# Two column groups of the last mixing sum in two-bank PSUM tiles, tile 32 in halves, five residual buffers, and a new order of the jobs

## The chip, the cores and the metric

The kernel runs on one core of a Trainium2 chip. Its time is the device time of one execution in microseconds; the time shown for the kernel before is the median of three runs. The profile is that of one more execution.

The names of the engines are those of the profile: PE is TensorE (PEld its weight loads), DVE VectorE, ACT ScalarE, POOL GpSimd, SP SyncE, which issues nearly all DMAs here.

## The reference

Two layers follow each other: a retention layer (attention with a decay in place of the softmax) over 8 batches, 8 heads, 576 positions and 64 dimensions a head, then a gated MLP with a mixing sum along the sequence.

```python
scores = scale * np.matmul(q, k.transpose(0, 1, 3, 2))
Dmat = np.where(rel >= 0, gamma[:, None, None] ** rel[None, :, :], 0.0)   # rel = pos[:, None] - pos[None, :]
attn = np.matmul(scores * Dmat[None], v)
x = attn.transpose(0, 2, 1, 3).reshape(B, S, H * D)      # (8, 576, 512)
h = gelu_tanh(x @ w_in)                                  # (8, 576, 1024)
u, v = h[..., :512], h[..., 512:]
v_n = (v - mean(v)) / np.sqrt(var(v) + 1e-06) * g_ln
v_s = np.einsum('ts,bsd->btd', w_sg, v_n) + b_sg[None, :, None]
out = x + (u * v_s) @ w_out
```

Inputs and output are float32.

## The kernel before

**Tiling.** Two batches form a pair (index p, 0 to 3). A pair has 1152 rows, nine tiles of 128 rows (index m; tile number i = 9p + m, 0 to 35). The retention layer runs in blocks (index b, five to a pair, 0 to 19): blocks of 256 positions of one batch, and one block in the middle of each pair (b mod 5 = 2) with the last 64 positions of the first batch and the first 64 of the second. Matmuls are in bf16, sums in float32 PSUM.

**The jobs.** The kernel is cut into some 940 jobs, each a short function on one engine. Those of a block are: loads of q, k and v (a_load, SP; q mostly for two blocks at once); scaling of q and v by powers of gamma and a cast of k (a_prep, POOL, but DVE and ACT for block 0); transposes of q and k on PE with a copy by DVE (a_T, a_Tev), or by DMA for the later blocks (a_TX, SP); scores (a_S, PE) and their product with a mask (a_Sev, DVE); the state K'V (a_Z, PE), its running sum (a_Zsum, DVE) and its copy (a_Zev, ACT); the output in two steps (a_O1 and a_O2, PE) and its copy to xT (a_Oev, ACT).

For each tile then: v = x w_in (m_V, PE), gelu (m_Vg, ACT), mean and variance (m_stats, DVE), reciprocal root (m_rs, POOL), normalising (m_norm, ACT); u = x w_in (m_U, PE) with gelu (m_Ug, ACT); for each batch bt and each of four column groups c the mixing sum (m_Wm opens it with the 64 rows of the shared middle tile, m_W adds four tiles; PE, each in two halves of 288 positions), its gate u * (sum + b) (m_Wg, DVE, a half at a time); at last the product with w_out (m_O, PE), the sum with the residual x (m_Oev, DVE) and the store (m_store, SP). The residual x of a tile is xT transposed back: on PE with a copy by ACT for the nine tiles of the first pair (m_XT, m_XTev), by DMA for the others (m_X).

**The order.** One constant (ORDER, L20 to L54) lists the numbers of the jobs in the order in which their instructions are issued; fN in it is a fill of N/2 matmuls on a tile of zeros (L210 to L217). Each engine executes its own jobs in this order and waits, in order, for what a job needs. So ORDER is the schedule of every engine and of the DMA queue of SP.

**Buffers.** BUFS (L126) gives their numbers: among others eight for loads (ld), four for output tiles (ob), two for the residual that PE transposes (xt). PSUM has eight banks: psP has two tiles of two banks each (transposes, scores and block outputs, tag pp), psD has four tiles of one bank (all others, tag d). The two halves of a mixing sum take two psD tiles.

**The opening.** rsrc (g_ln and b_sg) is transposed (to_col, L742) and worked on by DVE (col_math, L747 to L750); its result colr scales w_sg (ACT, L272, five jobs), which is then transposed on PE (build_wT, L760, ten jobs). w_in comes in two halves, each cast by DVE (L246) and ACT (L248). The load of w_sg reuses the buffer of the first half of w_in and so stands behind both casts. Before the change, SP loads q, k of block 0, q of block 1, v of block 0, k of block 1, the first half of w_in, v of block 1, the last rows of w_sg, q and k of block 2; the only fill is f4, ahead of the first build_wT.

**The end.** The last batch is bt = 7. Its four column groups run in the order c = 1, 2, 3, 0, each m_Wm directly ahead of its m_W. Then come tiles 34, 33, 35 (in two halves of 256 columns, L690 and L1004), 31 and 32.

The lines of the mixing sum:

```python
for half in range(2):
    cur["wp", b, c, half] = psD.tile([128, HS], F32, name="wp", tag="d")
```

Of the kernel before, what the change touches and what calls it, by code (L numbers as in the profile page):

```python
# [11 lines left out]
F32 = mybir.dt.float32  # L12
# [81 lines left out]
def kernel(  # L94
# [32 lines left out]
                xr=5, xt=2, pp=2, d=4)  # L127
# [530 lines left out]

    def m_Wm(b, c):
        p, e = divmod(b, 2)  # L660
        for half in range(2):
            cur["wp", b, c, half] = psD.tile([128, HS], F32, name="wp", tag="d")
        for g in range(2):
            for half in range(2):
                R, G = slice(64 * half, 64 * half + 64), slice(64 * g, 64 * g + 64)
                mid = vns[NT * p + MID] if half == e else vsw[p]
                nc.tensor.matmul(cur["wp", b, c, half][G, :], mid[R, 128 * c + 64 * g:128 * c + 64 * g + 64], wM[e][R, :],  # L667
                                 start=True, stop=False, skip_group_check=True)

    def m_W(b, c):  # L670
        p, e = divmod(b, 2)
        t0 = NT * p + (MID + 1 if e else 0)
        for half in (1, 0):
            ps = cur["wp", b, c, half]
            for j in range(MID):
                ins = nc.tensor.matmul(ps[:], vns[t0 + j][:, 128 * c:128 * c + 128], wT[e][:, j, half * HS:(half + 1) * HS],  # L676
                                       start=False, stop=(j == MID - 1), skip_group_check=True)
                if half and j == 0:
                    mark(ins, ("W", b, c))
        fence(ins, ("W", b, c))  # L680

    def m_Wg(b, c, half):
        p, e = divmod(b, 2)
        o = e * S + half * HS
        dst = uTs[p][:, c, o:o + HS]
        ins = nc.vector.scalar_tensor_tensor(dst, cur.pop(("wp", b, c, half))[:], colr[:, c:c + 1], dst, op0=Alu.add, op1=Alu.mult)  # L686
# [3 lines left out]
    LAST = NT * NP - 1  # L690
# [190 lines left out]
    for b in range(NBL):  # L881
# [77 lines left out]
        if n in (2, NBK - 1):  # L959
# [10 lines left out]
            for u in order:  # L970
                due = base + PR["WS"] * cum / tot
                if u[0] == "W":
                    c = u[1]
                    cum += 1090.0
                    db = Buf("d"), Buf("d")
# [8 lines left out]
                    for hf in range(2):  # L984
                        J["Wg", bt, c, hf] = add("DVE", 450.0, due + 400.0, lambda a=(bt, c, hf): m_Wg(*a),
                                                 deps=[jW] + list(dict.fromkeys(J["Ug", i, c] for i in tls)),
                                                 uses=[db[hf], B_u])
                else:
# [15 lines left out]
                    for hf in (0, 1) if i == LAST else (None,):  # L1004
# [38 lines left out]
```

## Time and profile before

| | |
|---|---|
| median of three runs | 207.51 us |
| the three runs | 204.18, 207.51, 210.31 us |
| the profiled execution | 206.49 us |
| its span | 204.8 us |
| PE busy | 182.8 us (89%) |
| DVE busy | 159.8 us (78%) |
| POOL busy | 115.6 us (56%) |
| ACT busy | 110.1 us (54%) |
| DMA | 50.47 MB, mean 246 GB/s |

The span is the time from the first to the last event of the profiled execution. An engine is busy while one of its instructions runs; waiting and the issue of DMAs are not counted. PE's matmuls are pipelined, so that the length of one row is longer than its share in a stream of them: a stream is read from the start of its first row to the start of the next group.

### The profile page before, as it was taken

How to read it: one execution, taken by the hardware profiler on the slowest of the kernel's cores; microseconds unless marked ns; L12 is line 12 of the kernel's file. 1: busy time of each engine (PE TensorE's matmuls, PEld its weight loads, DVE VectorE, ACT ScalarE, POOL GpSimd, SP SyncE). 2: the span in 40 equal slices, each digit the busy share in tenths (PEclk: the TensorE clock that was granted, in tenths of full speed). 3: DMA queues.
4: the chain of work that ended last, by engine and by line, in shares of the span. 5: the costliest groups of instructions: out<-in, count | busy, mean ns of one | idle time of the engine just before them, and what ended most of it. 6: DMA issues, size and time to landing. Idle time of an engine off the chain costs nothing.

```text
span 204.8 us, 7667 instructions
## 1 busy us (share of the span) xinstructions
PE 182.8 (89%) x3267; PEld 121.9 (60%) x3295; DVE 159.8 (78%) x295; ACT 110.1 (54%) x197; POOL 115.6 (56%) x163
## 2 busy tenths in 40 slices
PE   0336898999999999999999999999999999999992
PEld 0335384876765777757656776556656676656550
DVE  3459686898998999799965867789796678966673
ACT  4322769646866854788464685634346467054200
POOL 8457079949797979966576695217068253202000
PEclk9999999999999999999999999999999999999999
DMA  5996999899999992979999979999999979583735
GB/s 167 348 366 159 358 360 300 256 327 287 299 327 239 333 352 55 196 228 345 331 291 166 210 227 187 198 221 243 326 367 147 270 174 241 156 157 110 223 105 207
DMA packets 94239, 50.47 MB, mean 246 GB/s; under 512 B 45360, under 2 KB 87612, under 8 KB 94204
## 3 DMA queue, kind: packets, MB, share of 16 engines
q1 hardware_dynamic: 94176, 49.97, 93.2%
q8 instruction: 26, 0.43, 0.8%
q14 instruction: 9, 0.07, 0.1%
q10 hardware_dynamic: 28, 0.01, 0.0%
HBM read 32.79 MB, written 9.44 MB: 206 GB/s over the span
## 4 chain that ended last, share of the span: by engine, by line
PE 70%; DVE 11%; DMA 7%; POOL 6%; issue 2%; ACT 1%; SPq 1%; DVEq 0%; POOLq 0%
PE wp L676 15%; PE hu L638 13%; PE op L701 12%; PE hv L597 12%; PE pp L532 5%; PE pp L450 4%; DVE ret L463 4%; DMA ld<-in_q_dram 3%; POOL qb L362 3%; PE wp L667 3%; DMA kT<-kb 3%; PE pp L399 2%; PE zp L486 2%; POOL vb L362 2%; DMA out_dram<-ob 1%
## 5 line engine op out<-in xcount | busy, mean ns | idle before, releaser
L362 POOL TENSOR_TENSOR vb<-ld,gpow 128x1024 bf16<-128x1024 f32 (+1 forms) x20 | 34.5, 1731 | 14.1 <-DMA ld<-in_v_dram 14.1
L463 DVE TENSOR_TENSOR ret<-pp,msk 128x1024 bf16<-128x1024 f32 x32 | 38.7, 1218 | 3.8 <-PE pp L450 3.6
L597 PE MATMUL hv<-w_in,xT 128*128 128x512 bf16 x127 | 36.0, 385 | 1.6 <-ACT xT L586 0.4
L638 PE MATMUL hu<-xT,w_in 128*128 128x256 bf16 (+1 forms) x320 | 36.2, 262 | 0.2 <-ACT zb L518 0.2
L676 PE MATMUL wp<-wT,vn 128*128 128x288 bf16 x256 | 36.4, 287 | 0.0
L686 DVE SCALAR_TENSOR_TENSOR uT<-wp,colr,uT 128x288 bf16<-128x288 f32 x64 | 30.4, 509 | 7.4 <-PE wp L676 7.3
L627 ACT ACTIVATE vn<-vg,mv 128x512 bf16<-128x512 f32 x36 | 28.7, 809 | 12.6 <-POOL mv L620 12.5
L701 PE MATMUL op<-w_out,uT 128*128 128x512 bf16 (+1 forms) x137 | 34.8, 373 | 0.7
L604 ACT ACTIVATE vg<-hv 128x512 f32<-128x512 f32 x36 | 21.2, 596 | 25.0 <-PE hv L597 16.5
L362 POOL TENSOR_TENSOR qb<-ldq,gpow 128x1024 bf16<-128x1024 f32 x14 | 26.5, 1902 | 10.9 <-DMA ldq<-in_q_dram 10.9
L638 PEld LDWEIGHTS <-w_in 128*128 128x128 bf16 x320 | 28.1, 98 | 7.2 <-issue 0.4
L586 ACT ACTIVATE xT<-pp 128x512 bf16<-128x512 f32 (+1 forms) x40 | 20.5, 550 | 20.2 <-PE pp L532 20.1
L612 DVE BATCH_NORM_STATS2 bst<-vg 128x6 f32<-128x512 f32 x36 | 24.6, 684 | 4.9 <-ACT vg L604 4.8
L676 PEld LDWEIGHTS <-vn 128*128 128x128 bf16 x256 | 22.8, 98 | 8.3 <-issue 0.9
L617 POOL TENSOR_SCALAR mv<-mv 128x2 f32<-128x2 f32 (+1 forms) x20 | 4.8, 240 | 38.0 <-DVE mv L613 31.1
L648 ACT ACTIVATE uT<-hu 128x512 bf16<-128x512 f32 x36 | 20.9, 594 | 8.1 <-PE hu L638 7.9
L730 DVE SCALAR_TENSOR_TENSOR ob<-op,col,xr 128x512 f32<-128x512 f32 (+1 forms) x28 | 20.1, 728 | 6.0 <-PE op L701 5.5
L701 PEld LDWEIGHTS <-uT 128*128 128x128 bf16 x148 | 13.9, 98 | 13.1 <-DVE uT L686 0.4
L597 PEld LDWEIGHTS <-xT 128*128 128x128 bf16 x144 | 13.3, 99 | 13.2 <-ACT xT L586 1.3
L618 POOL TENSOR_TENSOR mv<-mv,mhalf 128x2 f32<-128x2 f32 (+1 forms) x20 | 13.7, 685 | 1.7
L352 POOL CAST kb<-ld 128x1024 bf16<-128x1024 f32 x14 | 14.3, 1037 | 0.6 <-DMA ld<-in_k_dram 0.6
L532 PE MATMUL pp<-qT,zb 64*64 64x128 bf16 (+1 forms) x256 | 11.6, 222 | 1.1 <-DVE ret L463 0.3
(85 smaller groups left out, 221.9 us busy)
## 6 DMA issues: line engine op xcount, KB each, us to landing
out_dram<-ob SPq DMA_DIRECT2D x35, 256.0 KB, 2.9
ld<-in_k_dram SPq DMA_DIRECT2D x16, 512.0 KB, 7.5
ld<-in_v_dram SPq DMA_DIRECT2D x16, 512.0 KB, 5.9
ldq<-in_q_dram SPq DMA_DIRECT2D x7, 1024.0 KB, 7.9
xT<-in_moe_w_sg_dram SPq DMA_DIRECT2D x2, 576.0 KB, 3.4
ld<-in_q_dram SPq DMA_DIRECT2D x2, 512.0 KB, 4.9
xT<-in_moe_w_in_dram SPq DMA_DIRECT2D x1, 1024.0 KB
ld<-in_q_dram SPq DMA_DIRECT2D x8, 128.0 KB, 5.5
```

The source lines that it names most:

```text
L362: ve.tensor_tensor(dst, src, g.unsqueeze(len(src.shape) - 1).to_broadcast(list(src.shape)), op=Alu.mult)
L463: ins = nc.vector.tensor_tensor(ret[:].rearrange("p r (k t) -> p (r k) t", k=2), sc[:].rearrange("p r (k t) -> p (r k) t", k=2), (msk2 if ...
L532: nc.tensor.matmul(ot[64 * c:64 * c + 64, bank, j * cs:(j + 1) * cs], lhsT, rhs, start=(bank, c) not in begun, stop=True, skip_group_check ...
L597: ins = nc.tensor.matmul(hv[:], xTs[p][:, m, kk, :], w_in[:, kk, F2:], start=(kk == 0), stop=(kk == KK - 1))
L604: unfence(nc.scalar.activation(vgs[i][:], cur.pop(("hv", i))[:], Act.Gelu_apprx_tanh), ("V", i))
L612: nc.vector.bn_stats(bst[:], vgs[i][:])
L627: nc.scalar.activation(vns[i][:], vg[:], Act.Identity, scale=mv[:, s, 2:3], bias=mv[:, s, 3:4])
L638: ins = nc.tensor.matmul(hu[:, n, :], w_in[:, kk, 128 * c:128 * c + 128], xTs[p][:, m:m + w, kk, :], start=(kk == 0), stop=(kk == KK - 1), ...
L648: unfence(nc.scalar.activation(uTs[p][:, c0:c1, 128 * m:128 * m + 128 * w], cur.pop(("hu", i, half))[:], Act.Gelu_apprx_tanh), ("U", i, half))
L676: ins = nc.tensor.matmul(ps[:], vns[t0 + j][:, 128 * c:128 * c + 128], wT[e][:, j, half * HS:(half + 1) * HS], start=False, stop=(j == MID ...
L686: ins = nc.vector.scalar_tensor_tensor(dst, cur.pop(("wp", b, c, half))[:], colr[:, c:c + 1], dst, op0=Alu.add, op1=Alu.mult)
L701: ins = nc.tensor.matmul(op[:], uTs[p][:, c, r], w_out[:, c, cs], start=(c == 0), stop=(c == KK - 1), skip_group_check=True)
```

## The change

In the last batch (bt = 7) the column groups c = 1 and c = 2 no longer take two one-bank tiles each but one two-bank tile of psP, one half in each bank, and one DVE instruction of 128 x 576 gates both halves. Their m_Wm stand further ahead in the order: before the O2 of block 19, and between the m_W of (6, 1) and the m_Wm of (6, 3). Tile 32 leaves in two halves of 256 columns like tile 35, with a job each for matmul, sum and store. The residual transposed by PE has five buffers in place of two. ORDER is new throughout; since the number of jobs changed, its numbers name other jobs from the last batch on.

In the new order of the opening, SP loads q, k, v of block 0, then q, k of block 1, the first half of w_in, q, k of block 2, v of block 1, the last rows of w_sg, v of block 2. A fill f14 (seven matmuls) is PE's first job and f6 stands behind block 0's scores; f4 is gone. POOL prepares v of block 0 first, then q and k of block 1, q and k of block 2, v of 1 and 2. DVE does the column math directly behind the first transposed copy, and the cast of w_in behind the transposed copy of block 1. On ACT four of the five w_sg scalings stand behind the copy of the state (1, 0), with the copies of the state and of the output of block 2 between them.

At the end PE works W(7, 1), the openers of (7, 0) and (7, 3), W(7, 2), W(7, 3), W(7, 0), then tiles 32 (two halves), 31, 34, 35 (two halves), 33. The gate of (7, 0) does half 0 first; before, it did half 1 first.

```diff
 ORDER = (
...
+    '0 f14 1 2 95 6 7 96 73 3 98 97 99 12 74 187 188 100 259 13 189 f6 260 262 190 263 101 8 261 103 264 104 265 17 '
...
     BUFS = dict(ld=8, ldq=2, qb=2, kb=2, vb=3, qT=2, kT=2, ret=4, zb=6, run=4, xT=2, uT=2, vg=3, mv=3, vn=14, ob=4,
-                xr=5, xt=2, pp=2, d=4)
+                xr=5, xt=5, pp=2, d=4)
...
+    WPP = ((2 * NP - 1, 1), (2 * NP - 1, 2))
+
     def m_Wm(b, c):
         p, e = divmod(b, 2)
+        if (b, c) in WPP:
+            cur["wp", b, c] = psP.tile([128, 2, 512], F32, name="pp", tag="pp")
         for half in range(2):
-            cur["wp", b, c, half] = psD.tile([128, HS], F32, name="wp", tag="d")
+            cur["wp", b, c, half] = (cur["wp", b, c][:, half, :HS] if (b, c) in WPP else
+                                     psD.tile([128, HS], F32, name="wp", tag="d")[:])
...
     def m_Wg(b, c, half):
         p, e = divmod(b, 2)
+        if half is None:
+            dst = uTs[p][:, c, e * S:e * S + S].rearrange("p (a w) -> p a w", a=2)
+            unfence(nc.vector.scalar_tensor_tensor(dst, cur.pop(("wp", b, c))[:, :, :HS], colr[:, c:c + 1], dst,
+                                                   op0=Alu.add, op1=Alu.mult), ("W", b, c))
+            return
...
-    LAST = NT * NP - 1
+    LAST = (NT * NP - 1, NT * NP - 4)
...
-                    db = Buf("d"), Buf("d")
+                    db = (Buf("pp"),) if (bt, c) in WPP else (Buf("d"), Buf("d"))
...
-                    for hf in range(2):
-                        J["Wg", bt, c, hf] = add("DVE", 450.0, due + 400.0, lambda a=(bt, c, hf): m_Wg(*a),
...
+                    if (bt, c) in WPP:
+                        J["Wg", bt, c, 0] = J["Wg", bt, c, 1] = add(
+                            "DVE", 770.0, due + 400.0, lambda a=(bt, c, None): m_Wg(*a),
+                            deps=[jW] + list(dict.fromkeys(J["Ug", i, c] for i in tls)), uses=[db[0], B_u])
+                    else:
+                        for hf in range(2):
+                            J["Wg", bt, c, hf] = add("DVE", 450.0, due + 400.0, lambda a=(bt, c, hf): m_Wg(*a),
...
-                    for hf in (0, 1) if i == LAST else (None,):
+                    for hf in (0, 1) if i in LAST else (None,):
```

The numbers 450.0 and 770.0 in it are weights of jobs that nothing reads any more; only ORDER decides.

More of the change, by code (lines that the diff above doesn't have):

```diff
@@ L675, in m_W @@
             for j in range(MID):
-                ins = nc.tensor.matmul(ps[:], vns[t0 + j][:, 128 * c:128 * c + 128], wT[e][:, j, half * HS:(half + 1) * HS],
+                ins = nc.tensor.matmul(ps, vns[t0 + j][:, 128 * c:128 * c + 128], wT[e][:, j, half * HS:(half + 1) * HS],
                                        start=False, stop=(j == MID - 1), skip_group_check=True)
@@ L683, in m_Wg @@
         p, e = divmod(b, 2)
+        if half is None:
[3 more added lines that the diff above has]
+            return
         o = e * S + half * HS
         dst = uTs[p][:, c, o:o + HS]
-        ins = nc.vector.scalar_tensor_tensor(dst, cur.pop(("wp", b, c, half))[:], colr[:, c:c + 1], dst, op0=Alu.add, op1=Alu.mult)
+        ins = nc.vector.scalar_tensor_tensor(dst, cur.pop(("wp", b, c, half)), colr[:, c:c + 1], dst, op0=Alu.add, op1=Alu.mult)
         cur["leftw", b, c] = cur.get(("leftw", b, c), 2) - 1
         unfence(ins, ("W", b, c), cur["leftw", b, c] == 0)
-    LAST = NT * NP - 1
+    LAST = (NT * NP - 1, NT * NP - 4)
     def m_O(i, hf=None):
@@ L983 @@
                     J["W", bt, c] = jW
-                    for hf in range(2):
-                        J["Wg", bt, c, hf] = add("DVE", 450.0, due + 400.0, lambda a=(bt, c, hf): m_Wg(*a),
-                                                 deps=[jW] + list(dict.fromkeys(J["Ug", i, c] for i in tls)),
-                                                 uses=[db[hf], B_u])
+                    if (bt, c) in WPP:
[5 more added lines that the diff above has]
+                            J["Wg", bt, c, hf] = add("DVE", 450.0, due + 400.0, lambda a=(bt, c, hf): m_Wg(*a),
+                                                     deps=[jW] + list(dict.fromkeys(J["Ug", i, c] for i in tls)),
+                                                     uses=[db[hf], B_u])
                 else:
```

65 rows, old and new, of the table ORDER are left out of this document.

## The prediction

> **What bounds the kernel now.** I read the busy times of stretches first, since an average over the span mixes three regimes. Columns: stretch, its length, busy us of PE, PEld, DVE, ACT and POOL, granted TensorE clock, DMA share, GB/s.
>
> ```profile
> 0.00:10.00 10.00, 1.55 (x45) 1.32 (x49) 4.03 (x17) 4.18 (x5) 6.21 (x26) 1.00 0.85 255
> 10.00:20.00 10.00, 5.07 (x184) 4.21 (x176) 7.36 (x11) 2.17 (x4) 7.21 (x6) 1.00 0.87 259
> 20.00:30.00 10.00, 8.79 (x183) 5.76 (x174) 7.60 (x16) 6.63 (x12) 3.04 (x6) 1.00 1.07 361
> ...
> 140.00:150.00 10.00, 9.89 (x184) 6.39 (x185) 8.32 (x15) 4.08 (x8) 3.56 (x5) 1.00 1.12 302
> ...
> 190.00:204.80 14.80, 10.56 (x75) 5.70 (x74) 9.05 (x16) 0.70 (x2) 0.00 (x0) 0.99 0.54 175
> ```
>
> The reader is to see that PE has no gap worth filling in the middle (9.89 of 10), that it idles 8.45 + 4.93 = 13.4 us in the first 20, and 4.2 us at the end. So a new order can win in three ways only: PE reaches its dense stretch earlier, the dense stretch holds less overhead, or the tail gets shorter. Then the chain of waits says what holds the opening and the tail (start, length, what):
>
> ```profile
> 7.94 1.90 POOL qb L362
> 9.84 1.87 POOL vb L362
> ...
> 13.38 2.26 DVE ret L463 x2
> 15.65 2.29 DVE w_in L246
> 17.93 1.13 DVE qT L414
> ...
> 21.18 0.61 PE hv L597
> ...
> 27.76 0.23 POOL mv L617
> ...
> 195.03 0.61 PE wp L676 x4
> ...
> 195.66 0.53 DVE uT L686
> ...
> 198.09 2.61 DMA out_dram<-ob
> 200.83 0.75 DVE ob L730
> ```
>
> The opening is a relay of POOL and DVE, not of PE: the first projection (hv) starts at 21.18 only.
>
> **The opening, step by step.** The new order changes what POOL and DVE do first. Here are the durations (timeline rows: start, length, instruction, idle time before it and what ended it):
>
> ```profile
> 7.38 1.03 PE L399 MATMUL pp<-ident,qb 64*128 64x64 bf16 x32 [0.57 <-ACT qb L350]
> ...
> 12.40 1.04 POOL L352 CAST qb<-ld 128x1024 bf16<-128x1024 f32 x1
> ...
> 12.96 0.42 DVE L514 TENSOR_TENSOR run<-zp,run 128x256 f32<-128x256 f32 x1
> ...
> 15.48 1.90 POOL L362 TENSOR_TENSOR vb<-ld,gpow 128x1024 bf16<-128x1024 f32 x1 [2.05 <-DMA ld<-in_v_dram]
> 15.56 2.37 DVE L246 CAST w_in<-xT 128x1024 bf16<-128x1024 f32 x1
> ...
> 17.34 1.49 POOL L362 TENSOR_TENSOR qb<-ld,gpow 128x512 bf16<-128x512 f32 x1
> ...
> 19.59 0.24 DVE L750 RECIPROCAL colr<-col 128x13 f32<-128x13 f32 x1
> ...
> 22.00 1.06 PE L597 MATMUL hv<-w_in,xT 128*128 128x512 bf16 x2 [0.22 <-issue]
> ...
> 23.64 0.69 DVE L414 COPY qT<-pp 128x1024 bf16<-128x1024 bf16 x1 [1.75 <-PE pp L399]
> ```
> ```profile
> 23.89 1.04 PE L597 MATMUL hv<-w_in,xT 128*128 128x512 bf16 x4
> ...
> 25.38 0.68 DVE L466 TENSOR_TENSOR ret<-pp,msk 128x512 bf16<-128x512 f32 x1
> 25.45 2.09 ACT L272 ACTIVATE wnat<-xT,colr 128x576 bf16<-128x576 f32 x3
> ...
> 25.98 0.68 DVE L612 BATCH_NORM_STATS2 bst<-vg 128x6 f32<-128x512 f32 x1
> ...
> 26.66 1.13 PE L216 MATMUL scr<-warm 128*128 128x256 f32 x4
> ...
> 27.63 1.28 PE L760 MATMUL wtp<-ident,wnat 128*128 128x128 bf16 x20
> ...
> 30.88 0.31 PE L486 MATMUL zp<-vb,qb 64*64 64x64 bf16 x8
> ...
> 31.69 0.38 ACT L518 ACTIVATE zb<-zp 128x256 bf16<-128x256 f32 x1 [0.42 <-DVE run L511]
> ...
> 35.02 0.64 PE L399 MATMUL pp<-ident,qb 64*128 64x64 bf16 x32 [0.28 <-POOL qb L362]
> ```
>
> *Warming matmuls.* The fill of 4 becomes one of 14 ahead of everything and one of 6 behind the first block's scores. The old fill was two matmuls, which the trace records as four: 1.13 us, so 0.28 a record at most, and I take 0.24 without the tail of the last. PE is slow at first: two hv took 1.06 at 22.00, four took 1.04 at 23.89, a factor 2, though the granted clock reads 1.00 from 20 to 30. The fill of 14 is seven matmuls or 14 records: 3.4 us all fast, 6.7 all slow, and less if steady work speeds PE up on the way, as the stretch from 19 to 23.9 did. They can begin near 1.2, so they end between 5 and 8; the transpose that follows them waited for ACT until 7.38 anyway. Fast, it takes 0.64 (row at 35.02) in place of 1.03. I let it end at 8.2 instead of 8.41; bounds 8.0 and 10.0. The fill of 6 is 1.4 us (2.9 slow) while PE waits for the next transpose's input, which POOL delivers at 12.8 (below): nothing. The old fill sat in front of transposes waiting for ACT's last w_sg row: its going is worth nothing either.
>
> *The relay.* v of block 0 is now loaded third and prepared first, q of block 1 after it. POOL: vb 7.94 to 9.8, qb to 11.7, k to 12.8. DVE: the qT copy (1.2) ends at 9.4, four column instructions of at most 0.24 at 10.3, first score product (1.13 to 1.2) 11.5, two running sums 12.4, second product 13.6 where it was 15.64, next qT 14.8 where it was 19.06. The w_in cast then starts at 14.8. In the old run it started at 15.56 beside a POOL multiply that ended at 17.38 and ended 0.55 later, so I let it end 0.55 behind the POOL multiply of 1.49 that is then running: 16.5, against 17.93. That lets the first hv start near 16.6 instead of 21.18, and the w_sg load go out (it stands behind that cast) at about 16.5 instead of 17.96.
>
> *What is late next.* The ten w_sg transposes (27.63) need all five ACT scalings of w_sg, the last of which ended at 25.45 + 2.09 = 27.54. In the new ACT line four of them stand behind a copy that waits for block 1's running sum on DVE. DVE from 16.5: product 1.2, qT 0.69, statistics 0.9, product 1.2, short product 0.68, sum 0.42 gives 21.6, and with 0.4 for ten hand-overs 22.0. ACT from there: copy 0.4, scaling 0.7, copy 0.4, scaling 0.7, an output copy of the same size 0.4, two scalings 1.4: 26.0. So the transposes start 1.6 earlier. Two small PE steps that stood behind them (Z of block 2, 0.31, and its O2, about as much) now come before: 0.6 more. **Opening: -2.2 us.** Bounds: 0 or slightly worse (transposes of block 0 ending at 10.0 give +1.6 and eat nearly all), and -4.1, if the lead of the statistics decides (27.76 before; by the same DVE line 23.6).
>
> [...]
>
> **The dense stretch.** The same matmuls in another order. What I can price is the change from full 128x128 tiles to 64-row work:
>
> ```profile
> 182.87 0.98 PE wp L676 x8
> ...
> 191.03 1.09 PE wp L676 x8
> ```
>
> Eight mixing matmuls take 0.98 followed by full tiles and 1.09 followed by small ones: 0.11 per change. Counted in the two orders from the first mixing job on, PE makes 45 such changes before and 39 after: 6 x 0.11 = **-0.6 us**. Bounds: 0, and twice that if the way back costs the same. Copies by ACT for nine residual tiles only move (five buffers for two): 0. On SP, block 14's k and v loads and the store queue pass others by up to a dozen places; PE's dense 9.89 says that these are covered, and the third rival prices them if not.
>
> **The tail.**
>
> ```profile
> 196.24 4.50 PE L701 MATMUL op<-w_out,uT 128*128 128x512 bf16 x23
> ```
> ```profile
> L686 DVE SCALAR_TENSOR_TENSOR uT<-wp,colr,uT 128x288 bf16<-128x288 f32 x64 | 30.4, 509 | 7.4 <-PE wp L676 7.3
> ```
>
> The two joint gates (c = 1 and 2 of the last batch) do 576 columns in one instruction. By the rows for 512 and 1024 columns (0.68 and 1.22) that is 0.75 against 2 x 0.509: 0.27 saved twice, on a DVE that waits for PE there, so 0 (-0.5 if it were late). Each now waits for both halves of its sum, but neither is the last gate. Their 64-row openers move up into PE's line beside others (their three saved changes are counted above); they hold both two-bank buffers, which after block 19's output nobody else asks for. Queued behind the first of them is block 19's O2; it needs the buffer of block 19's first score tile, whose DVE product lies about eight PE jobs back: 0.
>
> The last sum, c = 0, is worked half 1 first. Before, half 1 was done at 195.03 + 0.61, its gate ran at 195.66, and tile 34, which needs half 1 only, started at 196.24. Now half 0 is gated first and tile 32, which needs half 0, goes first: the gate starts after all eight matmuls, 4/8 of 0.98 later. **+0.5 us.** Five tiles' worth of output matmuls follow in both (4.50). The last write in the old run waited for a store (198.09 + 2.61 = 200.70) as well as for PE (196.24 + 4.50 = 200.74), and both ended together. Now the fifth tile reuses the buffer of tile 32, whose halves leave first: -0.1. The last tile is whole in both, so 0.75 of DVE and the store behind it stay. The extra store and the four extra, half as long matmuls cost SP and PEld, neither of which is last: 0. **Tail: +0.4.**
>
> **Sum.** -2.2 - 0.6 + 0.4 = -2.4. The profiled execution took 206.49 (span 204.8, 1.7 around it): 204.1. It lies 1.0 below the median shown (207.51 of 204.18 to 210.31), from which -2.4 gives 205.1; I take the middle, 204.6.
>
> **Rivals.**
> 1. The whole lead of the statistics comes through, and every second change saves both ways: -4.1 - 1.2 + 0.4 = -4.9, 201.6. For it: all four engines are early after 16.5. Against: ACT has one line, and four scalings wait in it.
> 2. The front gives nothing: PE is slow throughout or drops back, the fill of 14 ends at 8 and the fill of 6 at 2.9 us length pushes the next transpose, or DMA (0.85 and 0.87 busy in the first 20 us, little to gain) sets the pace of the loads. Then -0.6 + 0.4: 206.3.
> 3. Slower, from POOL's line. The new order puts the reciprocal root for tiles 16 and 17 straight behind half of block 13's q, and leaves PE ten jobs instead of seventeen between V(17) and the mixing sum that needs both tiles. PE takes its jobs in order, so a late q load stops everything. POOL has waited so already, though for block 13's q (95.23) only 0.36:
>
> ```profile
> 95.23 3.76 POOL L362 TENSOR_TENSOR qb<-ldq,gpow 128x1024 bf16<-128x1024 f32 x2 [0.36 <-DMA ldq<-in_q_dram]
> ```
> ```profile
> 150.46 1.90 POOL L362 TENSOR_TENSOR qb<-ldq,gpow 128x1024 bf16<-128x1024 f32 x1 [6.74 <-DMA ldq<-in_q_dram]
> ```
>
> The cover that is left is two mixing sums (2.1), a V (1.04), an output tile (0.8) and some 1 us of small steps, about 5; behind V(17) come gelu, statistics, root and two scalings, which fill it. Every us that q comes late counts in full: 204.1 + 6.7 = 210.8 with a wait like this one. It decides from about 2.4 us of delay on. Against it: the 0.36 above, and that the front moves the loads up too.
>
> **How the numbers follow.** Forecast 0.47, first rival 0.20, second 0.20, third 0.13. A measurement of this kernel tells about 2% from no change, 4.1 us. Below 202.4 lie most of the first rival and a little of the forecast: 0.25. Above 210.6 lies the far half of the third: 0.08. The rest, 0.67, is within 2%. The range 201.6 to 208.0 reaches from the first rival to 1.5 us above the second, and leaves out the third's long waits and what is beyond the first.
>
> **What would show it.** Right: hv first at 16 to 18 us, w_sg transposes from 26, PE idle in the first 20 us under 8 (the fill counts as busy), PE busy 9.8 or more of 10 from 40 to 190, tile 32 first about 0.65 us after the last sum. Wrong: w_sg transposes at 27.5 or later (second rival); a PE gap of over 1 us near 95 to 105 ended by ACT's vn (third); the chain of waits going through the joint gates or through SP at the end.

## The result and the profile after

| | before | after |
|---|---|---|
| median of six runs | 207.63 us | 212.76 us |
| all runs | 204.18 to 211.09 | 210.67 to 217.07 |
| profiled execution (span) | 206.49 (204.8) | 214.43 (212.7) |
| first mixing matmul on full tiles, W(0,0) | 42.44 us | 45.54 us |
| first matmul of the last output tiles | 196.24 us | 204.23 us |

Jobs are written without their prefix: W(0,0) is m_W of batch 0 and column group 0, T(3,q) the transposes of q of block 3, S(3,0) the first scores of that block, swap(0) the copies m_swap of the first pair.

The change made the kernel slower: ratio 1.028, 95% interval 1.021 to 1.035. Ratios here and below compare undisturbed executions only, medians are over all of them, so the two can differ by a per cent or more. The profiled execution of after lies 1.7 us above its median and that of before 1.1 us below, so the 7.9 us between the two profiles are more than the change costs: 2.8% is 5.8 us.

The page of after, first the busy times, then the busy tenths of PE and its granted clock in 40 slices, then the DMA queues:

```profile
PE 191.7 (90%) x3315; PEld 127.8 (60%) x3315; DVE 163.5 (77%) x294; ACT 111.3 (52%) x197; POOL 115.3 (54%) x163
...
PE   7776699669999969998999989999999999999982
...
PEclk9999769969999999999999999999999999999998
...
q8 instruction: 26, 0.43, 0.8%
```

Two things are new. The clock, 1.00 in all rows of the old run but the last (0.99), is down in two places. And PE, which had no gap worth filling after 40 us, has some. The stretches between show where (columns as in the prediction):

```profile
20.00:22.50 2.50, 1.01 (x52) 0.75 (x51) 2.40 (x5) 0.46 (x3) 1.56 (x2) 1.00 0.99 350
22.50:25.00 2.50, 1.85 (x70) 1.15 (x62) 0.90 (x3) 2.50 (x5) 1.38 (x4) 0.77 1.07 374
25.00:27.50 2.50, 1.94 (x17) 1.76 (x18) 1.17 (x4) 2.50 (x6) 0.53 (x1) 0.50 1.08 412
27.50:30.00 2.50, 2.50 (x15) 1.40 (x13) 1.13 (x3) 0.94 (x2) 2.50 (x2) 0.50 1.10 345
...
40.00:42.50 2.50, 0.66 (x6) 0.21 (x4) 2.47 (x2) 2.50 (x6) 2.50 (x2) 1.00 1.12 353
42.50:45.00 2.50, 0.46 (x20) 0.46 (x24) 1.99 (x2) 0.20 (x1) 2.50 (x2) 0.87 0.98 292
45.00:47.50 2.50, 2.50 (x32) 1.41 (x24) 2.27 (x2) 0.00 (x0) 1.95 (x3) 0.50 0.90 209
```

PE is thin from 20 to 25 us (1.01 and 1.85 us busy of 2.5), its clock is halved from 25 to 30. It nearly stands still from 40 to 45, and is at half clock again behind that. The timeline of all engines says what it waited for there:

```profile
39.40 1.90 POOL L362 TENSOR_TENSOR vb<-ld,gpow 128x1024 bf16<-128x1024 f32 x1
39.60 1.84 DVE L656 COPY vn<-vn 64x512 bf16<-64x512 bf16 x1
...
41.26 3.86 POOL L362 TENSOR_TENSOR qb<-ldq,gpow 128x1024 bf16<-128x1024 f32 x2
41.48 1.88 DVE L657 COPY vn<-vn 64x512 bf16<-64x512 bf16 x1
41.50 0.31 PE L672 MATMUL wp<-wM,vn 64*64 64x288 bf16 x3 [1.15 <-DVE vn L656]
...
43.28 1.21 DVE L414 COPY kT<-pp 128x2048 bf16<-128x2048 bf16 x1
44.54 1.07 PE L450 MATMUL pp<-qT,kT 64*64 64x128 bf16 x32 [2.73 <-DVE kT L414]
45.54 2.10 PE L681 MATMUL wp<-wT,vn 128*128 128x288 bf16 x8
```

The same place before the change:

```profile
38.56 0.41 DVE L656 COPY vn<-vn 64x512 bf16<-64x512 bf16 x1
...
38.99 0.29 DVE L657 COPY vn<-vn 64x512 bf16<-64x512 bf16 x1
...
40.50 1.90 POOL L362 TENSOR_TENSOR vb<-ld,gpow 128x1024 bf16<-128x1024 f32 x1
...
42.44 1.14 PE L676 MATMUL wp<-wT,vn 128*128 128x288 bf16 x8
```

L656 and L657 are the two half-tile copies of swap(0), which exchange the halves of the pair's middle tile for the mixing sums. They took 0.41 and 0.29 us before, and were done 1.2 us ahead of POOL's multiply. Here each ends about when POOL's multiply beside it ends. The kT copy of block 3 stands behind them on DVE, in both orders, and the scores S(3,0) and S(3,1) and the sum W(0,0) behind that on PE.

Later in the run PE pauses twice in the middle of a series of equal matmuls, and the profile names nothing that it waited for ("issue"). The rows at 99.25 and 204.23 are two other waits, for DVE:

```profile
77.33 0.64 PE L399 MATMUL pp<-ident,kb 64*128 64x64 bf16 x31
...
79.68 0.20 PE L399 MATMUL pp<-ident,kb 64*128 64x64 bf16 x1 [1.71 <-issue]
...
99.25 0.42 PE L450 MATMUL pp<-qT,kT 64*64 64x128 bf16 x16 [0.85 <-DVE qT L414]
...
128.04 0.28 PE L486 MATMUL zp<-vb,kb 64*64 64x64 bf16 x11 [1.19 <-issue]
...
204.23 4.51 PE L711 MATMUL op<-w_out,uT 128*128 128x256 bf16 x28 [0.61 <-DVE uT L696]
```

From W(0,0) to the first of the last output tiles it takes 158.7 us; before, 153.8. Each of these is one execution.

### The profile page after: what moved, and what is told of

Its sections match the earlier page's. It is cut to its first block, busy times and chain, and to the rows that moved or that the text cites. A ratio compares the mean times of both kernels' runs of the same rounds, so it can differ in the third digit from the quotient of the medians.

```text
span 212.7 us, 7748 instructions
## 1 busy us (share of the span) xinstructions
PE 191.7 (90%) x3315; PEld 127.8 (60%) x3315; DVE 163.5 (77%) x294; ACT 111.3 (52%) x197; POOL 115.3 (54%) x163
## 4 chain that ended last, share of the span: by engine, by line
PE 74%; DVE 10%; DMA 5%; issue 4%; ACT 3%; POOL 2%; SPq 1%; DVEq 0%; POOLq 0%
PE wp L681 14%; PE op L711 14%; PE hu L638 14%; PE hv L597 12%; PE pp L532 5%; PE pp L450 4%; DMA ld<-in_v_dram 3%; DMA xT<-in_moe_w_sg_dram 3%; PE wp L672 2%; PE zp L486 2%; PE pp L399 2%; PE wtp L770 2%; DVE vn L657 2%; DVE ret L463 2%; ACT wnat L272 1%
## 5 line engine op out<-in xcount | busy, mean ns | idle before, releaser
L597 PE MATMUL hv<-w_in,xT 128*128 128x512 bf16 x144 | 37.1, 387 | 0.1
L696 DVE SCALAR_TENSOR_TENSOR uT<-wp,colr,uT 128x288 bf16<-128x288 f32 x60 | 28.6, 509 | 8.8 <-PE wp L681 7.9
L681 PE MATMUL wp<-wT,vn 128*128 128x288 bf16 x240 | 34.7, 292 | 0.0
L681 PEld LDWEIGHTS <-vn 128*128 128x128 bf16 x256 | 23.5, 99 | 8.6 <-issue 0.7
L711 PEld LDWEIGHTS <-uT 128*128 128x128 bf16 x152 | 14.4, 98 | 13.7 <-DVE uT L696 1.1
L450 PE MATMUL pp<-qT,kT 64*64 64x128 bf16 x448 | 11.1, 225 | 3.8 <-DVE kT L414 2.7
```

What stands on the lines that cost most here:

```text
L597: ins = nc.tensor.matmul(hv[:], xTs[p][:, m, kk, :], w_in[:, kk, F2:], start=(kk == 0), stop=(kk == KK - 1))
L681: ins = nc.tensor.matmul(ps, vns[t0 + j][:, 128 * c:128 * c + 128], wT[e][:, j, half * HS:(half + 1) * HS], start=False, stop=(j == MID - ...
L711: ins = nc.tensor.matmul(op[:], uTs[p][:, c, r], w_out[:, c, cs], start=(c == 0), stop=(c == KK - 1), skip_group_check=True)
```

## The experiments

Theories: 1, swap(0) beside POOL's multiplies is the loss. 2, the clock that falls after the thin stretch at 20 to 25 us. 3, the new order of the later stages. 4, the joint gates and halves themselves. A fifth came up on the way. "Opening" is the time of W(0,0), "dense" from there to the first of the last output matmuls, both of the profiled execution; the ratio, with its 95% interval, is to runs of the kernel before beside it (their medians: 206.98 to 208.22 us).

| kernel | median | ratio | opening | dense |
|---|---|---|---|---|
| before | 207.63 | 1 | 42.44 | 153.8 |
| after | 212.76 | 1.028 (1.021 to 1.035) | 45.54 | 158.7 |
| structure alone | 207.54 | 0.995 (0.990 to 1.001) | 42.44 | 158.1 |
| swaps on ACT | 210.17 | 1.008 (1.002 to 1.013) | 40.48 | 162.9 |
| kT first | 212.79 | 1.011 (0.997 to 1.026) | 40.99 | 158.2 |
| two more fills | 210.50 | 1.000 (0.992 to 1.007) | 40.21 | 159.0 |
| new opening only | 211.10 | 1.013 (1.004 to 1.022) | 46.06 | 155.8 |
| new rest only | 210.62 | 1.016 (1.011 to 1.021) | 42.78 | 158.9 |
| fills, new opening, old rest | 205.62 | 0.986 (0.977 to 0.996) | 39.62 | 155.0 |
| half a block shifted | 213.73 | 1.018 (1.004 to 1.031) | 41.94 | 162.4 |
| three stores left out | 208.74 | 1.007 (1.001 to 1.012) | 40.50 | 156.6 |
| before, half a block shifted | 209.84 | 1.015 (1.006 to 1.024) | 42.27 | 158.8 |
| fills, new opening, kT first, old rest | 208.38 | 1.004 (0.999 to 1.008) | 41.30 | 161.2 |
| fills, new opening, swaps on ACT, old rest | 206.11 | 1.002 (0.998 to 1.005) | 40.77 | 156.2 |

One profile can lie off its kernel's median: that of the structure alone took 210.67 and has two waits of its own, 1.11 us for a DMA of kT and 1.27 us for ACT's gelu. Its dense stretch is 158.1 us in the order that took 153.8 before, at the same median. So a difference of some us between two dense stretches proves nothing by itself; the ratios count.

### Structure alone

The old order of jobs, with joint gates, halves of tile 32 and five residual buffers.

> The order of before with the structure of the change alone: joint gates for (7,1) and (7,2) in two-bank PSUM tiles, tile 32 in halves, five residual buffers. All theories that put the loss in the order (1, 2, 3) expect the time of before, 207.6, plus at most 0.5 us, with the swaps of before (0.29 us a copy) and W(0,0) near 42.4. Theory 4 (the joint gates and halves cost): 208.5 or more, with the excess between the last W and the end, 1 us over the 8.56 us from the first of the last final products to the end.

207.54, ratio 0.995 (0.990 to 1.001): the structure costs nothing that shows. Theory 4 falls, and the loss is in the order.

### Swaps on ACT

```diff
-        nc.vector.tensor_copy(vsw[p][NB0:, :], was[:NB0, :])
-        nc.vector.tensor_copy(vsw[p][:NB0, :], was[NB0:, :])
+        nc.scalar.activation(vsw[p][NB0:, :], was[:NB0, :], Act.Copy)
+        nc.scalar.activation(vsw[p][:NB0, :], was[NB0:, :], Act.Copy)
```

> The changed kernel with the two half-tile copies of each swap on ACT in place of DVE; nothing else moves in the order. Theory 1 (the stall at 40 to 45 us is DVE's two copies of swap(0), 1.84 and 1.88 us beside POOL's multiplies against 0.41 and 0.29 before, with the kT copy and W(0,0) queued behind them): the 2.73 us idle before S(3,0) and the 1.15 us idle inside Wm(0,0) go, the granted clock stays at 1.0 in 45 to 50, W(0,0) starts near 41.5 in place of 45.54, and the time is 208.0 to 209.5. Theory 2 (the clock that falls to 0.50 after the thin PE stretch at 20 to 25 us is what costs): the clock still falls at 25 to 30 here, the time is 211 to 213. Theory 3 (the loss is spread over the new order of the later stages): at most 2 us come back, 211 to 212.

The stall at 40 to 45 went as theory 1 says: W(0,0) at 40.48, although the clock still fell (0.72 from 20 to 25 us, 0.60 from 25 to 30). But the median is 210.17, between the theories. In the profiled execution, which took 213.56, the lead was lost again later, in a pause at the very place of after, now 3.93 us long and followed by a granted clock of 0.50 from 77.5 to 80 us.

```profile
72.24 0.64 PE L399 MATMUL pp<-ident,kb 64*128 64x64 bf16 x31
76.80 0.23 PE L399 MATMUL pp<-ident,kb 64*128 64x64 bf16 x1 [3.93 <-issue]
```

### kT first

In the order list, by the jobs' names:

```diff
+a_Tev(3, k)
 m_swap(0)
...
-a_Tev(3, k)
...
+a_S(3, 0)
+a_S(3, 1)
 m_Wm(0, 0)
-a_S(3, 0)
...
-a_S(3, 1)
```

> The changed kernel with the copy of kT of block 3 ahead of swap(0) in DVE's order, and S(3,0), S(3,1) ahead of Wm(0,0) on PE. Theory 1: the swap copies still take 1.8 us each where a POOL multiply runs beside them, but only W(0,0) waits for them: S(3,0) starts near 41 in place of 44.54, W(0,0) near 43.5, and the time is 210 to 211. Theory 2 and theory 3: within 1 us of the changed kernel's 212.8, as the order of four instructions changes neither the fall of the clock at 25 us nor the later stages.

W(0,0) came at 40.99, sooner than theory 1 expected (43.5): with kT ahead, swap(0) started at 40.02, 0.37 us before POOL's next multiply, and took 0.29 us a copy in place of the 1.8 expected. On the time the four runs, from 209.36 to 217.26, decide nothing: the interval of the ratio is 0.997 to 1.026. The dense stretch, 158.2 us, is as long as in after.

### Two more fills

In the order list, where f4 is a fill of two matmuls:

```diff
+f4
 a_Z(2)
...
+f4
 a_O1(2)
```

> The changed kernel with two more fills of four blank matmuls (some 0.9 us each), ahead of a_Z(2) and ahead of the first product O1(2), in the stretch from 20 to 22.5 us where PE is busy for 1.01 of 2.5 us. Theory 2: the granted clock stays at 1.0 from 22.5 to 31, the wT transposes and hv products there run at full speed, T(3,q) comes 1.5 to 2.5 us sooner than 34.80, and the time falls by as much, to 210.5 to 211.5. Theory 1: the clock stays up and T(3,q) comes sooner, but swap(0) and the kT copy behind it still wait for POOL's multiplies, which do not move, so W(0,0) stays near 45 and the time within 1 us of 212.8.

The clock stayed at 1.00 from 20 to 30 us and T(3,q) came at 33.04 in place of 34.80, as theory 2 says. Theory 1 was wrong on what follows: swap(0) went ahead of the multiply and was not held at all.

```profile
25.00:30.00 5.00, 4.48 (x73) 3.35 (x63) 3.23 (x8) 4.75 (x9) 3.14 (x2) 1.00 1.10 371
```
```profile
37.84 0.29 DVE L656 COPY vn<-vn 64x512 bf16<-64x512 bf16 x1
38.16 0.29 DVE L657 COPY vn<-vn 64x512 bf16<-64x512 bf16 x1
...
39.19 1.90 POOL L362 TENSOR_TENSOR vb<-ld,gpow 128x1024 bf16<-128x1024 f32 x1 [1.23 <-DMA ld<-in_v_dram]
39.64 0.64 PE L450 MATMUL pp<-qT,kT 64*64 64x128 bf16 x32 [1.03 <-DVE kT L414]
40.21 1.03 PE L681 MATMUL wp<-wT,vn 128*128 128x288 bf16 x7
```

So the two causes are one chain. POOL's multiply starts at 39.19 here, when its v has landed, and at 39.40 in after, straight behind POOL's own work; in after the swap, 1.76 us later than here, came 0.2 us behind it. Either link can be taken out: with the swaps on ACT, W(0,0) came at 40.48 under the slow clock, and here it comes at 40.21. Yet this kernel, with W(0,0) where the prediction had it, is no faster than before (ratio 1.000, median 210.50). The pause in T(8,k) is there again, 1.38 us, but at another matmul:

```profile
72.84 0.52 PE L399 MATMUL pp<-ident,kb 64*128 64x64 bf16 x23
74.74 0.32 PE L399 MATMUL pp<-ident,kb 64*128 64x64 bf16 x9 [1.38 <-issue]
```

Eight matmuls sooner. The two fills are eight matmuls in the trace. This gave the fifth theory: PE runs out of instructions. The page of after counts 26 packets on the queue called instruction, 0.43 MB or some 16.5 KB each, and PE has 3315 matmuls and as many weight loads: 6630 instructions, 255 to a packet. With the few other instructions of PE a block is put at 256, an estimate from these counts that the trace of after bears out: in steps of 256 instructions from the pause at 79.68, 25 of the 26 packets start to come in 0.1 to 4.3 us after PE has entered the block ahead of them.

### New opening only, and new rest only

The new order list up to and with m_W(0, 0), then the jobs that are left in the old order; and the other way round.

> The new order up to and with the first mixing sum W(0,0), the order of before from there on (structure of the change kept). Theory 1 (all of the loss arises before W(0,0)): 212 to 213, as the changed kernel. Theory 3 (the later order loses 4 to 5 us whatever the opening does): from W(0,0) to the first of the last final products it takes the 153.8 us of before, in place of 158.7, no idle of PE over 0.7 us put down to issue after 50 us, and the time is 207 to 209, as W(0,0) comes between 41 and 45.

> The order of before up to and with W(0,0), the new order from there on. Theory 1: 207 to 208, as W(0,0) stands at 42.4 and the swap copy at 0.3 us as before. Theory 3: W(0,0) at 42.4, then 158 to 159 us to the first of the last final products, with PE pausing for 0.3 to 4 us in the last transposes of T(8,k) and again some 48 us later in Z, both put down to issue, 0.85 us before S(10) ended by DVE's qT copy: 211 to 213.

Both halves lose: 1.013 and 1.016, together 1.029, the 1.028 of the change. The first repeats swap(0) beside POOL (1.86 and 1.88 us for 1.84 and 1.88, the same 2.73 us idle before S(3,0)). Its time, 211.10, fits neither theory (212 to 213, and 207 to 209), as W(0,0) came later than either had it, at 46.06. It has no pause put down to issue over 0.28 us, and its dense stretch is 155.8 (153.8 were expected; half clock around W(0,0) is in it). The second opens like before and needs 158.9. Its pause of 1.59 us fell on the hv matmuls at 78.96, not in T(8,k), for its opening has fewer instructions; its second, 0.80 us at 126.22, is put down to ACT's gelu, which ended 0.1 us before; but it stands at a block's end too, with the block landed 1.4 us before as in the pauses put down to issue, so which of the two held PE is open. The 0.85 us for qT came: swap(1) again, 1.01 us beside a POOL multiply.

```profile
94.17 1.05 POOL L362 TENSOR_TENSOR vb<-ld,gpow 128x512 bf16<-128x512 f32 x1 [2.76 <-PE pp L532]
94.35 1.01 DVE L656 COPY vn<-vn 64x512 bf16<-64x512 bf16 x1
...
96.77 0.42 PE L450 MATMUL pp<-qT,kT 64*64 64x128 bf16 x16 [0.85 <-DVE qT L414]
```

### Half a block shifted

Two more fills as above, and in the fill f6:

```diff
+            for _ in range(64 * (n == 6)):
+                nc.tensor.matmul(scr[:64, :64], ident[:64, :64], ident[:64, :64], start=True, stop=True, skip_group_check=True)
```

> The kernel with the two added fills, and 64 blank 64x64 matmuls more at the opening fill (128 instructions of PE, ahead of the second scores, where PE waits anyway). Theory 5 (the pauses that the profile puts down to issue are PE waiting for its next 16 KB of instructions, so they stand at fixed counts of PE's instructions): T(8,k) runs its 32 transposes without a pause, and each pause that is left stands 64 matmuls earlier in PE's order than one in the kernel without them, or at another of the places 256 instructions apart; the time stays within 1.5 us of 210.5, as other blocks become the short ones. Rival (the pauses come from the work itself: a port, a PSUM buffer, a semaphore that the profile does not show): T(8,k) pauses at the same place, x23 and x9 or x31 and x1, for 0.3 to 4 us as in the four runs before.

T(8,k) ran through, and the pauses stood elsewhere, the largest in the outputs of block 5 at 63.47:

```profile
63.47 0.75 PE L534 MATMUL pp<-ret,vb 64*64 64x128 bf16 x16 [2.82 <-issue]
...
79.69 0.64 PE L401 MATMUL pp<-ident,kb 64*128 64x64 bf16 x32
```

The next one, 1.19 us at 131.07, lies ten blocks on (1277 loads between the two, and a matmul with each). So the place follows the count, and the rival falls. The expected time was missed: 213.73, above the 210.5 plus 1.5. In this profile W(0,0) came 1.7 us later, the pauses are 4.0 us against 3.2 without the shift (0.81, 1.38 and 1.01), and the long one halved the clock behind it: 0.55, 0.50 and 0.59 in the three stretches of 2.5 us from 62.5 on, where PE was busy for 6.3 us. That is worth some 2.9 us by an estimate from these rows. So the shifted boundaries were worse ones in this execution.

### Before, half a block shifted

The old kernel, with the lines of the last edit for n == 2, and in its order list:

```diff
+f2
 a_T(1, q)
```

> The kernel before, with 66 blank matmuls (132 instructions of PE) ahead of the second T(1,q), in 2.27 us of idle time of PE; nothing else. Theory 5 as a matter of where the blocks of 256 instructions fall (the old order is free of pauses because its blocks end at quiet places of the DMA queue): at least one pause of 0.3 us or more put down to issue after 45 us, where before has none, and 208 to 210.5. Rival (only the new order, with its small matmuls closer together, runs PE out of instructions): no such pause, and the time of before within 0.7 us.

As theory 5 says: the old order, free of pauses, now has one of 0.89 and one of 1.14 us, and 1.5% more time, while W(0,0) did not move (42.27). The two pauses are 2.0 of the 5.0 us that the dense stretch is longer; three more waits, 0.65 to 0.75 us each for POOL and ACT, are another 2.1.

```profile
45.72 0.64 PE L534 MATMUL pp<-ret,vb 64*64 64x128 bf16 x30 [0.89 <-issue]
...
62.81 0.35 PE L534 MATMUL pp<-ret,vb 64*64 64x128 bf16 x6 [1.14 <-issue]
```

Between the two, the stretch view counts 384 matmuls and 383 loads, three blocks of 256 but for one; in the kernel with the swaps on ACT, from the pause at 125.76 to that at 161.04, 512 loads, which with a matmul each is four:

```profile
45.70:62.80 17.10, 15.95 (x384) 10.76 (x383) 15.16 (x25) 11.09 (x20) 13.19 (x13) 1.00 1.05 305
```
```profile
125.75:161.03 35.28, 34.23 (x504) 21.89 (x512) 28.17 (x51) 18.66 (x34) 17.69 (x26) 1.00 1.14 251
```

### Three stores left out

In the kernel with the two more fills:

```diff
     def m_store(i, hf=None):
+        if i in (0, 2, 3):
+            return
```

> The kernel with the two added fills (new order throughout), with the stores of tiles 0, 2 and 3 left out: 0.75 MB less of output is written, and those rows of the output are not. These three stores stand together in the new order's DMA queue, between 68.48 and 72.04 us, and the 16 KB of instructions that PE ran out of came in at 72.37, 3.79 us after PE had passed the block before. Theory 5 with the queue as its cause (the block of instructions waits for the data transfers ahead of it): it comes in within 2.5 us of the place where it came 3.79 us after, T(8,k) runs its 32 transposes without the pause of 1.38 us, and the span falls by 1 to 1.5 us against 207.7. Rival (the block is asked for late, or takes long for a reason of PE's own): it still comes near 3.8 us after, and the pause stays at 0.3 to 1.7 us.

The block came in 1.68 us after PE had passed the boundary ahead of it, in place of 3.79, T(8,k) had no pause, and the span is 2.1 us shorter (1 to 1.5 expected).

```profile
72.26 0.64 PE L399 MATMUL pp<-ident,kb 64*128 64x64 bf16 x32
```

So with less data in the queue this block came sooner, as foretold, in the one execution that was profiled. The time did not fall with it: the ratio is 1.007 without the stores and 1.000 with them, so what this pause is worth in most runs is not shown. How full the DMA engines are at this place can be read for after, in which PE passed the boundary at 73.18; the line below is the 5 us from 73 to 78 in 40 slices, and the next block started to come in at 77.50:

```profile
DMA  9999999999999999999999997989999999999978
...
q8 instruction: 1, 0.02, 1.2%
```

### Fills, new opening, old rest; and two variants

> The new order up to W(0,0) with the two added fills that keep the clock up, the order of before from there on. Theory 3 with theory 2: W(0,0) at 40 to 41 (40.2 in the kernel with the fills and the new order throughout), then the 153.8 us of before and its 8.56 us of end: a span of 202.5 to 203.5 and a time of 204.3 to 205.5, under the 207.9 of before. Theory 1 alone: the swap copies still run into POOL's multiplies and W(0,0) stays at 44 to 45.5: 208 or more.

W(0,0) at 39.62, span 202.9, time 205.62 (204.3 to 205.5 expected): 0.986 of before, from only four runs (0.977 to 0.996), the fastest version here. Times the 1.016 of the new rest this gives 1.002, and the kernel with both, that with two more fills, has 1.000.

> The new order up to W(0,0) with the two added fills, the order of before from there on, and the kT copy of block 3 ahead of swap(0), with both scores of block 3 ahead of the first half-size matmuls of W(0,0). In the kernel without the last edit PE waited 0.97 us for that kT copy at 39.04. Theory: that wait falls to 0.3 us or less, W(0,0) comes 0.3 to 0.6 us sooner than 39.62, and the time is 204.5 to 205.5, 1.0 to 1.5 % under that of before. Rival: swap(0), now later, meets POOL's multiply and W(0,0) waits for it: W(0,0) at 41 or later, 206.5 to 208.

The rival won, with W(0,0) at 41.30 and 208.38. kT, now first, moved the swap 0.14 us behind the start of POOL's multiply:

```profile
38.95 1.90 POOL L362 TENSOR_TENSOR vb<-ld,gpow 128x1024 bf16<-128x1024 f32 x1 [1.12 <-DMA ld<-in_v_dram]
39.09 1.91 DVE L656 COPY vn<-vn 64x512 bf16<-64x512 bf16 x1
...
41.03 1.88 DVE L657 COPY vn<-vn 64x512 bf16<-64x512 bf16 x1
```

> The new order up to W(0,0) with the two added fills, the order of before from there on, and all swap copies on ACT, where no multiply of POOL can hold them (0.63 us a copy in the kernel that had them on ACT before). If the meeting of DVE's swap copies with POOL's multiplies (late by 0.14 us: 1.91 and 1.88 us a copy; in time: 0.29 us) is what makes W(0,0) swing between 39.6 and 45.5, then W(0,0) stands at 39.5 to 40.5 here, followed by 153.8 to 155 us to the first of the last final products: a span of 202 to 203.5 and a time of 204 to 205.5, 1 to 1.5 % under before, with less spread than the 204.6 to 210.5 of the version with the copies on DVE. Rival: ACT's copies delay the norms and gates that stand behind them on ACT, and the stretch after W(0,0) takes 157 us or more: 207 or more.

Eleven of twelve runs fell between 205.5 and 208.1 and one at 210.39, so that a smaller spread than the 204.64 to 210.52 of four runs is not shown, and the time is that of before (ratio 1.002). W(0,0) was 0.3 us later than expected and the dense stretch 1.2 us longer: two new pauses for instructions, 0.93 us inside the scores of block 3 and 1.48 us at 46.94, where the next block started to come in 4.0 us after its boundary (40.25 to 44.23).

## Why the prediction was wrong

**The opening, right up to the w_sg transposes, in part by luck.** Fill of 14: block 0's transposes ran at 7.34 for 0.64 (1.03 before, without the fill), end 7.98 (8.2 predicted). First hv at 15.24 (16.6): the w_in cast took 0.68 while POOL waited (2.37 before, beside a POOL multiply). PE was idle for 5.2 of the first 20 us (under 8). The w_sg transposes, of which three ran from 24.14 on, began in earnest at 25.85 (26.0). That this agrees although hv was 1.4 early is luck: DVE stood still for 1.85 us ahead of the next transposed copy (18.12), for transposes that waited for POOL, and POOL had waited 3.47 us for ACT's cast of w_in. The prediction had none of this.

```profile
0.00:10.00 10.00, 7.41 (x92) 5.73 (x96) 4.74 (x22) 4.18 (x5) 6.34 (x26) 1.00 0.86 256
10.00:20.00 10.00, 7.36 (x197) 4.45 (x182) 7.80 (x12) 5.04 (x9) 6.06 (x6) 1.00 1.02 287
```
```profile
15.24 1.08 PE L597 MATMUL hv<-w_in,xT 128*128 128x512 bf16 x3
...
25.85 2.53 PE L770 MATMUL wtp<-ident,wnat 128*128 128x128 bf16 x22 [0.38 <-ACT wnat L272]
```

**The first step that failed: "Opening: -2.2 us".** "So the transposes start 1.6 earlier" came true (25.85 for 27.63), but the lead did not reach W(0,0), which was to come at 40.2 and came at 45.54: +3.1 in place of -2.2. The sum put nothing for what lies between. T(3,q) was 1.76 us later than with the fills (34.80 against 33.04), which is the slow clock; from there to W(0,0) it took 10.74 against 7.17, which is swap(0). Together 5.3. Neither part stands alone: in four executions in which the clock fell, T(3,q) was 0.9 to 2.3 us later than with the fills, and in the two of them where the swap was not held, W(0,0) still came at 40.48 and 40.99. The slow clock is what the second rival warned of, but the rival was priced as the loss of the lead alone, and what the delay would run into was not asked. The granted clock read 0.77 from 22.5 to 25 us and 0.50 from 25 to 30, although PE's longest pause from 20 to 25 us was 0.89 us; how long or how thin a stretch must be for that, no run shows. For the second part, the prediction had the row of a DVE cast held by a POOL multiply (15.56) and used it for that one cast. The copies of swap(0) took 0.29 or 0.41 us where they started ahead of POOL's multiply, and 1.84 to 1.91 where they started 0.14 to 0.22 us behind the start of one; what holds them, no run here shows.

**The second step that failed: "The same matmuls in another order", -0.6.** Between the two profiles it is +4.9; by the ratio of the new rest alone, 1.016, it is +3.3 (2.3 to 4.4). The price per change of tile size was not what decided. What the sum left out are waits of PE that come with the order. The profile of after has pauses of 1.71 and 1.19 us for instructions, 0.85 us behind swap(1), and the half clock around W(0,0), with 0.50 for 2.5 us in 45 to 47.5, worth about 1.2. These are 5 us in that one execution; smaller gains and losses beside them were not separated, and the pauses differ from one execution to the next (that in T(8,k) took 0.32, 1.38, 1.71 and 3.93 us in four kernels). The new rest alone, at full clock, shows that most of the loss does not hang on the opening.

**The tail, +0.4: right.** PE waits 0.61 for the gate of half 0 in place of 0.12 (+0.5 predicted), and from there to the end it takes 8.46 in place of 8.54 (-0.1 predicted). The joint gates, predicted at 0.75, took 0.82 and were not last.

**Rival 3** did not come: the scalings of q waited for their loads for 2.7 us in all of the run, 2.2 us at most, and none of the stalls of PE ended with one.

**Left open.** What sets the wait of a block of instructions at a given place, beyond the one case of the three stores; how long the pauses are in most runs, as each kernel has one profile; and how much of the 1.6% of the new rest they make up.

## What to carry to other kernels

Before moving a DVE copy in a hand-made order, look which POOL instruction will start within a microsecond of it, and what stands behind the copy on DVE: starting 0.14 us behind a multiply made two copies 3.2 us longer here. Look at thin stretches of PE ahead of dense work: here one with 1.01 of 2.5 us busy was followed by 0.50 of the clock from 25 to 30 us, and two fills in it kept the clock at 1.00. In a kernel of thousands of small matmuls, count PE's instructions between loads: 64 blank matmuls more at the front moved the largest pause from 74.74 to 63.47 here, so compare orders by runs and not by their job lists, and when PE pauses for "issue" in the middle of a series, count from pause to pause.

## What the runs showed of the hardware

PE's instructions come in blocks: 26 packets of some 16.5 KB in after. Between two pauses of one run lie 767 matmuls and loads (before, half a block shifted), 512 loads (swaps on ACT) or 1277 loads (half a block shifted), with a matmul to each load 3, 4 and 10 times 256 to within six. In the two such pauses of after, PE went on 1.2 us after the block had landed (78.45 and 79.68, 126.80 and 128.04). The blocks of after took 0.9 to 1.6 us to move, and the one ahead of the pause of 1.71 us started 4.3 us after PE had passed the boundary ahead (73.18 to 77.50); with the swaps on ACT it was 6.3 us (68.09 to 74.38), ahead of the pause of 3.93. At its two pauses in after, PE was through its 256 instructions in 4.8 and 4.1 us, and the blocks that started 4.3 and 2.9 us after the boundary came too late. The two longest pauses, 2.82 us (half a block shifted) and 3.93 us (swaps on ACT), each had a granted clock of 0.50 behind them; behind that of 1.71 us in after it read 1.00. In T(8,k) the pauses took 0.3 to 3.9 us a time.
